# Attention scores of batches 2 to 7: three products of fp16 halves in place of one fp32 product

## The chip, the cores and the metric

The kernel runs on one core of a Trainium2 chip. The metric is the device time of one execution in microseconds (us), as the median of several runs. A profile of one more execution says what each engine did when. Engines are TensorE (PE; its weight loads are listed apart, as PEld), VectorE (DVE), ScalarE (ACT), GpSimd (POOL) and SyncE (SP, which issues the DMAs).

## The reference

Attention over a band of 65 keys and 32 global keys, with 32 global queries that see everything, is followed by a two-layer feed-forward part on all tokens. Cut to what matters:

```python
B, H, SL, SG, D = 8, 8, 512, 32, 64                       # inputs q_l, k_l, v_l, q_g, k_g, v_g
s_g   = q_g @ concat(k_g, k_l).T / 8                      # global queries, all 544 keys
out_g = softmax(s_g) @ concat(v_g, v_l)
s_ll  = where(|i - j| <= 32, q_l @ k_l.T / 8, -1e9)       # local queries, band
out_l = softmax(concat(q_l @ k_g.T / 8, s_ll)) @ concat(v_g, v_l)
x = concat(out_g, out_l).transpose(0, 2, 1, 3).reshape(B * 544, 512)
h = x @ w_in                                              # 512 -> 2048
out = (h * cos(h)) @ w_out                                # 2048 -> 512
```

The queries and keys are scaled up (factors 5.7 to 8), so the scores need more precision than one fp16 product gives.

## The kernel before

**Precision.** Nearly every product runs on PE as three products of fp16 halves: a value `x` is scaled by a power of two and split into `hi = fp16(x)` and `lo = fp16(x - hi)`, and `hi*hi + hi*lo + lo*hi` is summed in PSUM. The scores alone are single fp32 products (`sc_a`, L536, and `g_a`, L693).

**Tiling.** A batch has 4 head pairs, the two heads on partitions 0 to 63 and 64 to 127. Per pair, four windows of 128 queries see 192 or 224 keys each: `sc_a` computes windows 0 and 1 into two PSUM tiles (one per head), then windows 2 and 3 into two more, so a pair has two score blocks `ps_b_p_0_h` and `ps_b_p_2_h`, each of 4 matmuls with 64 rows of contraction. The global queries of two pairs are done together, in `gps_b_g_0` (288 keys) and `gps_b_g_1` (256 keys), 4 matmuls of 32 columns each.

**A pair's way.** SP loads queries and keys (`qkr_b_p`, three buffers); PE makes the scores `ps`; DVE scales them by -1/8, adds the mask and takes the row minimum (`sc_b`, tile `t`); ACT takes the exponential (`sc_c`); DVE the reciprocals (`sm`); ACT and DVE write the fp16 halves (`planes`, `sc_d`); SP transposes these by DMA (`pt`); PE multiplies them by the values (`acc`); ACT and DVE write the halves of the result (`xh`, `xl`).

**The feed-forward part** goes by chunks `c` of 256 tokens (two per batch) and 8 elements `j` per chunk: PE `ph_c_j` (24 matmuls of 256 columns), ACT `u`, DVE `u`, ACT `w` (sine), POOL `w*w`, DVE `gf`, ACT `gh` (fp16), POOL `gl` (the rest in fp16), and three elements later PE `po` (12 matmuls of 512 columns). There are three PSUM buffers for `ph`: `ph` of an element needs `gf` of the element three before it.

**Order.** `at(slot, phase, f, ...)` puts each step into a slot (one slot per element of the feed-forward part, 16 per batch); `steady` gives the slots of a pair of batches 2 to 7 relative to a slot `t`, which moves by 4 from pair to pair. A scheduler then orders each engine's instructions by these priorities. Every engine works through its own list strictly in order. In the names below, `ps_5_1_2_0` is batch 5, pair 1, windows 2 and 3, head 0; `u_8_4` is chunk 8, element 4. Attention of batch 5 runs beside the feed-forward part of batch 4 (chunks 8 and 9).

## Time and profile before

| what | value |
|---|---|
| three runs | 951.33, 949.33, 951.34 us (median 951.33) |
| the profiled execution's own time | 949.26 us |
| its span, first to last instruction | 947.5 us |
| PE / PEld / DVE / ACT / POOL busy | 95% / 63% / 61% / 70% / 45% |

The span is some 1.8 us shorter than the execution's own time; this lies outside of the instructions. Busy PE says that matmuls are in flight, not that the array is at its peak: matmuls overlap, so the cost of one is read from the distance between the starts of two.

### The profile page before, as it was taken

The numbers are of one execution on the slowest core, as the hardware profiler recorded it, in microseconds if no ns is written. First come the engines' busy times: TensorE is split into PE (matmuls) and PEld (weight loads), VectorE is DVE, ScalarE is ACT, GpSimd is POOL, SyncE is SP. The second block draws the span as 40 slices with busy tenths as digits, with TensorE's granted clock in tenths as the row PEclk, the third lists the DMA queues.
The fourth block names the chain that finished last, engine by engine and source line by source line (L and its number), as shares of the span: only waits on it lengthen the run. The fifth ranks groups of instructions, "written<-read, shape, count | busy, mean of one in ns | idle before, by whom it ended". The sixth has DMA issues, their size and how long they took to land.

```text
span 947.5 us, 19962 instructions
## 1 busy us (share of the span) xinstructions
PE 896.2 (95%) x7643; PEld 597.5 (63%) x7643; DVE 578.5 (61%) x1568; ACT 660.6 (70%) x1419; POOL 421.9 (45%) x508
## 2 busy tenths in 40 slices
...
GB/s 366 389 133 192 82 149 153 130 122 134 43 118 48 154 53 96 85 123 112 65 116 56 179 46 134 46 160 38 117 57 92 62 68 59 24 1 24 1 23 23
DMA packets 155176, 96.41 MB, mean 102 GB/s; under 512 B 141000, under 2 KB 141128, under 8 KB 153288
## 3 DMA queue, kind: packets, MB, share of 16 engines
...
## 4 chain that ended last, share of the span: by engine, by line
PE 82%; DVE 7%; ACT 3%; POOL 3%; DMA 2%; issue 1%; SPq 0%; ACTq 0%; POOLq 0%
PE ph L812 36%; PE po L872 35%; PE ps L536 5%; PE acc L654 4%; PE gps L693 2%; DVE planes L602 1%; PE gacc L748 1%; DMA raw_wo<-wo 1%; DMA vr<-v 1%; ACT t L434 1%; POOL wo_hl L222 1%; POOL vl L518 1%; DVE z_wo L241 1%; POOL wi_l L222 1%; DVE raw_wi L241 1%
## 5 line engine op out<-in xcount | busy, mean ns | idle before, releaser
L872 PE MATMUL po<-wo_hl,gh 128*128 128x512 f16 x1088 | 321.8, 380 | 9.7 <-POOL wo_hl L222 9.7
L812 PE MATMUL ph<-xh,wi_h 128*128 128x256 f16 x1024 | 280.4, 274 | 3.3 <-DVE gf L852 3.3
L812 PE MATMUL ph<-xl,wi_h 128*128 128x256 f16 x1024 | 279.8, 273 | 0.5 <-DVE xl L675 0.5
L812 PE MATMUL ph<-xh,wi_l 128*128 128x256 f16 x1024 | 279.8, 273 | 0.0
L222 POOL TENSOR_TENSOR gl<-gf,gh 128x512 f16<-128x512 f32 (+1 forms) x184 | 173.8, 955 | 230.2 <-ACT gh L856 229.3
L222 POOL TENSOR_TENSOR w<-w 128x512 f32<-128x512 f32 (+1 forms) x184 | 152.9, 841 | 248.3 <-ACT w L434 236.0
L812 PEld LDWEIGHTS <-wi_h 128*128 128x128 f16 x2176 | 206.0, 98 | 56.2 <-issue 19.6
L872 PE MATMUL po<-wo_hl,gl 128*128 128x512 f16 x544 | 201.5, 381 | 0.0
L872 PEld LDWEIGHTS <-gh 128*128 128x128 f16 x1088 | 106.8, 98 | 103.0 <-issue 2.3
L856 ACT CAST gh<-gf 128x512 f16<-128x512 f32 x136 | 83.3, 613 | 123.8 <-DVE gf L852 122.8
L852 DVE SCALAR_TENSOR_TENSOR gf<-w,ph 128x512 f32<-128x512 f32 x136 | 93.0, 684 | 113.7 <-POOL w L222 113.0
L434 ACT ACTIVATE w<-u,ca 128x512 f32<-128x512 f32 x136 | 97.9, 721 | 87.5 <-DVE u L835 84.8
L835 DVE SCALAR_TENSOR_TENSOR u<-u,cm,ph 128x512 f32<-128x512 f32 x136 | 101.2, 744 | 94.5 <-ACT u L834 94.5
L434 ACT ACTIVATE t<-t,mn 128x192 f32<-128x192 f32 (+1 forms) x256 | 116.6, 456 | 6.4 <-DVE mn L554 6.0
L812 PEld LDWEIGHTS <-wi_l 128*128 128x128 f16 x1088 | 106.7, 98 | 14.2 <-issue 1.4
L602 DVE SCALAR_TENSOR_TENSOR planes<-t,sm,planes 128x192 f16<-128x192 f32 (+1 forms) x232 | 100.4, 493 | 13.9 <-ACT planes L601 13.2
L834 ACT ACTIVATE u<-ph,cm 128x512 f32<-128x512 f32 x136 | 92.0, 677 | 18.8 <-PE ph L812 18.8
L872 PEld LDWEIGHTS <-gl 128*128 128x128 f16 x544 | 53.3, 98 | 73.0 <-issue 10.7
L554 DVE CUSTOM_DVE_ANT_0 t<-ps,msk 128x192 f32<-128x192 f32 (+1 forms) x256 | 82.8, 366 | 11.4 <-PE ps L536 10.4
L601 ACT ACTIVATE planes<-t,sm 128x192 f16<-128x192 f32 (+1 forms) x232 | 86.1, 455 | 2.2 <-DVE gsm L720 2.2
L536 PE MATMUL ps<-qkr 64*128 64x192 f32 (+1 forms) x496 | 73.0, 382 | 6.1 <-DMA qkr<-qf 5.4
L434 ACT ACT_TABLE_LOAD x58 | 74.4, 1283 | 3.7 <-DVE u L835 2.0
...
## 6 DMA issues: line engine op xcount, KB each, us to landing
qkr<-qf SPq DMA_DIRECT2D x31, 608.0 KB, 5.0
vr<-v SPq DMA_DIRECT2D x8, 1280.0 KB, 6.6
...
```

The lines of the kernel that those rows point to most:

```text
L222: nc.gpsimd.tensor_tensor(o[..., c], a[..., c], b[..., c], op=op)
L434: ins = nc.scalar.activation(*a, **k).ins
L536: nc.tensor.matmul(pt[h][:, c], q[r, QZ[j] : QZ[j] + P], k[r, z : z + w], start=True, stop=True, skip_group_check=True,)
L554: nc.vector.tensor_tensor_reduce(t[:, h], pt[h], msk[:, MOFF[i] : MOFF[i] + w], NAL, 3.0e38, ALU.add, ALU.min, mn[:, h : h + 1],)
L601: a = nc.scalar.activation(hi, t[:, h], AF.Identity, scale=r)
L602: d = nc.vector.scalar_tensor_tensor(lo, t[:, h], r, hi, op0=ALU.mult, op1=ALU.subtract)
L812: nc.tensor.matmul(ph[:, a], w[:, kc, f], x[:, kc, q], start=first and ip == 0, stop=last and ip == 2, skip_group_check=True,)
L834: nc.scalar.activation(u, ph, AF.Identity, bias=m)
L835: nc.vector.scalar_tensor_tensor(u, u, m, ph, op0=ALU.subtract, op1=ALU.subtract)
L852: nc.vector.scalar_tensor_tensor(gf, w, 0.5, st.pop(("ph", c, j)).rearrange("p a b -> p (a b)"), op0=ALU.subtract, op1=ALU.mult,)
L856: nc.scalar.copy(gh, gf)
L872: nc.tensor.matmul(po[k], g[:, a * CT + k * P : a * CT + (k + 1) * P], w[:, 2 * j + a], start=(j == 0 and i == 0), stop=(j == NS - 1 and i ...
```

## The change

For batches 2 to 7 the scores become three products of fp16 halves. What is added per pair:

- `q_m` (DVE): the largest absolute value per partition over queries and keys together, 1216 columns, into a bf16 column `qm`.
- `q_p` (PE): one matmul of that column with a constant matrix of ones. It sums the 128 maxima into a bound that all partitions get. It writes into one extra column of the PSUM tile of the score block two windows earlier, of the pair before (`host`), so it needs no PSUM tile of its own.
- `q_s` (DVE): five instructions on one column each, from the bound to a power-of-two scale and to the factor that takes the place of -1/8 in `sc_b` and `g_b`.
- `q_h`: ACT writes the upper half `qh` (1216 columns, fp16), DVE the lower half, in place over `qkr`.
- `sc_a` and `g_a`: three matmuls for one, the products outermost and the heads innermost.

The slots of a pair move: its load starts two slots earlier relative to `t` (-12 for -10), the first score block and the first global block one slot later (-6 for -7, -5 for -6), the load of the values one slot earlier (-13 for -12). The other new names in the diff (`SQ`, `GLE`, `WLE`, `WPT`, `WIS`, `PSQ`, `PSG`, `GB`, `LG`, `U1S`, `VDS`) hold what the expressions that they replace gave, and are left out here.

```diff
+FB = 2
+QB = 2
+QH = "A"
-s_load = -10
-s_sc0 = -7
+s_load = -12
+s_qm = -10
+s_qh = -8
+s_sc0 = -6
-s_gs0 = -6
+s_gs0 = -5
-s_v = -12
+s_v = -13
...
         def sc_a(b, p, i):
...
+            nb, np_ = (b, p + 1) if p < 3 else (b + 1, 0)
+            host = i == 2 and FB <= nb < B
+            pt = [
+                ps.tile([P, w0 + w1_ + (1 if host and h == 0 else 0)], F32, tag="att", name=f"ps_{b}_{p}_{i}_{h}")
+                for h in range(2)
+            ]
+            if host:
+                st["pmq", nb, np_] = pt[0][:, w0 + w1_ :]
+            if b >= FB:
+                qh, ql, kh, kl = st["qk", b, p]
+                for j, c in ((i, slice(0, w0)), (i + 1, slice(w0, w0 + w1_))):
+                    z, w = WIN[j]
+                    for n, (q, k) in enumerate(((qh, kh), (qh, kl), (ql, kh))):
+                        for h in range(2):
+                            r = slice(D * h, D * h + D)
+                            nc.tensor.matmul(
+                                pt[h][:, c], q[r, QZ[j] : QZ[j] + P], k[r, z : z + w], start=n == 0, stop=n == 2,
+                                skip_group_check=True,
+                            )
...
+        def q_m(b, p):
+            raw = st["raw_qk", b, p]
+            m = mp.tile([P, 1], BF16, tag="qm", name=f"qm_{b}_{p}")
+            nc.vector.tensor_reduce(
+                m, raw.rearrange("p a b -> p (a b)"), axis=AX.X, op=ALU.max, apply_absolute_value=True
+            )
...
+        def q_p(b, p):
+            nc.tensor.matmul(
+                st["pmq", b, p], ones13, st.pop(("qm", b, p)), start=True, stop=True, skip_group_check=True
+            )
...
+        def q_h(b, p):
+            raw, s = st.pop(("raw_qk", b, p)), st["qs", b, p][0]
+            hi = mp.tile([P, 2, NZ], F16, tag="qh", name=f"qh_{b}_{p}", bufs=QB)
...
+            if QH == "A":
+                nc.scalar.activation(hi, raw, AF.Identity, scale=s)
+            else:
+                nc.vector.tensor_scalar(hi, raw, s, None, op0=ALU.mult)
+            nc.vector.scalar_tensor_tensor(lo, raw, s, hi, op0=ALU.mult, op1=ALU.subtract)
...
         def attn_pair(b, p, o):
             if b:
                 at(o["load"], PJ, load_qk, b, p)
+            if b >= FB:
+                at(o["load"] + s_qm - s_load, PG, q_m, b, p)
+                h = o["host"]
+                at(h, PC, q_s, b, p)
+                at(max(h, o["load"] + s_qh - s_load), PF, q_h, b, p)
             attn_rest(b, p, o)
```

How the order of the engines moves is shown at three places, all while chunk 8 and the attention of batch 5 run.

PE, the first score block of pair 2 of batch 5. Before, from the last `po` matmul ahead of it to the `ph` behind it:

```order
L872 LDWEIGHTS gl_8_1_7009
L872 MATMUL po_8_1_7118<-wo_hl_88,gl_8_1_7009 128x512
L536 MATMUL ps_5_2_0_0_7242<-qkr_5_2_7005 128x192
L536 MATMUL ps_5_2_0_1_7243<-qkr_5_2_7005 128x192
L536 MATMUL ps_5_2_0_0_7242<-qkr_5_2_7005 128x224
L536 MATMUL ps_5_2_0_1_7243<-qkr_5_2_7005 128x224
L812 LDWEIGHTS wi_h_86
L812 MATMUL ph_8_5_7287<-xh_4_5803,wi_h_86 128x256
```

Now, the same place, the three products of its first window (192 columns):

```order
L969 MATMUL po_8_1_7631<-wo_hl_88,gl_8_2_7595 128x512
L558 LDWEIGHTS qh_5_2_7699
L558 MATMUL ps_5_2_0_0_7840<-qh_5_2_7699 128x192
L558 LDWEIGHTS qh_5_2_7699
L558 MATMUL ps_5_2_0_1_7841<-qh_5_2_7699 128x192
L558 LDWEIGHTS qh_5_2_7699
L558 MATMUL ps_5_2_0_0_7840<-qkr_5_2_7295,qh_5_2_7699 128x192
L558 LDWEIGHTS qh_5_2_7699
L558 MATMUL ps_5_2_0_1_7841<-qkr_5_2_7295,qh_5_2_7699 128x192
L558 LDWEIGHTS qkr_5_2_7295
L558 MATMUL ps_5_2_0_0_7840<-qh_5_2_7699,qkr_5_2_7295 128x192
L558 LDWEIGHTS qkr_5_2_7295
L558 MATMUL ps_5_2_0_1_7841<-qh_5_2_7699,qkr_5_2_7295 128x192
```

The three products of the second window follow in the same way, heads in turn. Then, in pairs 0 and 2, come the three products of window 2 for head 0 alone; those for head 1 follow only behind the next `ph` and `po`. The block now stands behind `ph_8_5`, where it stood ahead of it.

DVE, from the last `planes` of pair 1 of batch 5 to `gf_8_3`. Before:

```order
L602 SCALAR_TENSOR_TENSOR planes3_82<-t_5_1_2_7071,sm_5_1_7182,planes3_82 128x192 x2
L720 TENSOR_SCALAR gsm_5_0_7191<-gsm_5_0_7191 128x1
L721 RECIPROCAL gsm_5_0_7191<-gsm_5_0_7191 128x1
L730 TENSOR_SCALAR gt_5_0_6959<-gt_5_0_6959,gsm_5_0_7191 128x544
L731 CAST planes_g_84<-gt_5_0_6959 128x544
L835 SCALAR_TENSOR_TENSOR u_8_4_7226<-u_8_4_7226,cm_8_6817,ph_8_4_7201 128x512
L852 SCALAR_TENSOR_TENSOR gf_8_3_7197<-w_8_3_7114,ph_8_3_7088 128x512
```

Now, to `gf_8_4`:

```order
L582 TENSOR_REDUCE qm_5_3_7862<-qkr_5_3_7717 128x1
L679 SCALAR_TENSOR_TENSOR planes3_82<-t_5_1_2_7574,sm_5_1_7706,planes3_82 128x192
L615 SCALAR_TENSOR_TENSOR qkr_5_2_7295<-qkr_5_2_7295,qs_5_2_7584,qh_5_2_7699 128x1216
L582 TENSOR_REDUCE qm_6_0_8246<-qkr_6_0_8065 128x1
L808 TENSOR_SCALAR gsm_5_0_7715<-gsm_5_0_7715 128x1
L923 SCALAR_TENSOR_TENSOR u_8_4_7752<-u_8_4_7752,cm_8_7298,ph_8_4_7727 128x512
L946 SCALAR_TENSOR_TENSOR gf_8_3_7723<-w_8_3_7627,ph_8_3_7601 128x512
L809 RECIPROCAL gsm_5_0_7715<-gsm_5_0_7715 128x1
L923 SCALAR_TENSOR_TENSOR u_8_5_7824<-u_8_5_7824,cm_8_7298,ph_8_5_7799 128x512
L818 TENSOR_SCALAR gt_5_0_7581<-gt_5_0_7581,gsm_5_0_7715 128x544
L819 CAST planes_g_84<-gt_5_0_7581 128x544
L946 SCALAR_TENSOR_TENSOR gf_8_4_7795<-w_8_4_7753,ph_8_4_7727 128x512
```

Two reductions `qm` and the lower half (written to `qkr_5_2`) have come in ahead of `u_8_4` and `gf_8_3`, and `u_8_5` stands ahead of `gf_8_4`. On ACT the same stretch before:

```order
L434 ACTIVATE gt_5_0_6959,gsm_5_0_7191<-gt_5_0_6959,gmn_5_0_6960 128x544
L434 ACT_TABLE_LOAD
L434 ACTIVATE w_8_3_7114<-u_8_3_7113,ca_8_6816 128x512
L834 ACTIVATE u_8_4_7226<-ph_8_4_7201,cm_8_6817 128x512
L434 ACTIVATE w_8_4_7227<-u_8_4_7226,ca_8_6816 128x512
L856 CAST gh_8_3_7194<-gf_8_3_7197 128x512
L856 CAST gh_8_4_7280<-gf_8_4_7283 128x512
L834 ACTIVATE u_8_5_7312<-ph_8_5_7287,cm_8_6817 128x512
L434 ACTIVATE w_8_5_7313<-u_8_5_7312,ca_8_6816 128x512
L856 CAST gh_8_5_7331<-gf_8_5_7334 128x512
```

And now:

```order
L612 ACTIVATE qh_5_2_7699<-qkr_5_2_7295,qs_5_2_7584 128x1216
L448 ACTIVATE gt_5_0_7581,gsm_5_0_7715<-gt_5_0_7581,gmn_5_0_7582 128x544
L448 ACT_TABLE_LOAD
L448 ACTIVATE w_8_3_7627<-u_8_3_7626,ca_8_7297 128x512
L922 ACTIVATE u_8_4_7752<-ph_8_4_7727,cm_8_7298 128x512
L922 ACTIVATE u_8_5_7824<-ph_8_5_7799,cm_8_7298 128x512
L448 ACTIVATE w_8_4_7753<-u_8_4_7752,ca_8_7297 128x512
L950 CAST gh_8_3_7720<-gf_8_3_7723 128x512
L448 ACTIVATE w_8_5_7825<-u_8_5_7824,ca_8_7297 128x512
L950 CAST gh_8_4_7792<-gf_8_4_7795 128x512
L950 CAST gh_8_5_7865<-gf_8_5_7868 128x512
```

`qh_5_2` is new, and `u_8_5` has moved ahead of `w_8_4`, so that two elements are under way at a time.

DVE, where the maximum of the next batch's values (`vm_6`) is taken. Before:

```order
L554 ISA t_5_1_2_7071,mn_5_1_3_7075<-ps_5_1_2_0_7060,msk_73 128x192
L554 ISA mn_5_1_3_7075 128x1
L490 TENSOR_REDUCE vm_6_7583<-vr_6_7448 128x1
L852 SCALAR_TENSOR_TENSOR gf_8_2_7084<-w_8_2_7041,ph_8_2_7015 128x512
L554 ISA t_5_1_2_7071,mn_5_1_2_7072<-ps_5_1_2_1_7061,msk_73 128x224
L554 ISA mn_5_1_2_7072 128x1
L554 ISA t_5_1_2_7071,mn_5_1_3_7075<-ps_5_1_2_1_7061,msk_73 128x192
L554 ISA mn_5_1_3_7075 128x1
L462 TENSOR_SCALAR d_v6_7585<-ident_64,vm_6_7583 128x128
L835 SCALAR_TENSOR_TENSOR u_8_3_7113<-u_8_3_7113,cm_8_6817,ph_8_3_7088 128x512
```

Now:

```order
L594 TENSOR_SCALAR qs_5_2_7584<-ps_5_1_2_0_7541 128x1
L946 SCALAR_TENSOR_TENSOR gf_8_2_7597<-w_8_2_7522,ph_8_2_7496 128x512
L505 TENSOR_REDUCE vm_6_8041<-vr_6_7913 128x1
L794 ISA gt_5_0_7581,gmn_5_0_7582<-gps_5_0_0_7556,zero_74,ng_5_0_6834 128x288
L794 ISA gmn_5_0_7582 128x1
L488 TENSOR_SCALAR qs_5_2_7584<-qs_5_2_7584 128x1
L650 TENSOR_SCALAR sm_5_1_7706<-sm_5_1_7706 128x8
L923 SCALAR_TENSOR_TENSOR u_8_3_7626<-u_8_3_7626,cm_8_7298,ph_8_3_7601 128x512
L477 TENSOR_SCALAR d_v6_8043<-ident_64,vm_6_8041 128x128
```

`gf_8_2` stood behind `vm_6` and stands ahead of it now.

## Rows read from the trace of the kernel before

**Rows 1.** The page's part 1: busy us, share of the span and instructions of each engine.

```profile
PE 896.2 (95%) x7643; PEld 597.5 (63%) x7643; DVE 578.5 (61%) x1568; ACT 660.6 (70%) x1419; POOL 421.9 (45%) x508
```

**Rows 2.** Busy time by windows, from 203 to 710 us. Columns: window, its length, then PE, PEld, DVE, ACT and POOL busy (instructions), the granted clock of TensorE, DMA share, GB/s.

```profile
203.00:710.00 507.00, 507.00 (x4484) 335.82 (x4483) 313.99 (x880) 371.98 (x824) 189.82 (x173) 1.00 0.44 97
```

**Rows 3.** Who waited for whom in that window: total us, times, longest us.

```profile
ACT gh L856 <- DVE gf L852: 62.5, 40, 3.9
DVE gf L852 <- POOL w L222: 57.3, 50, 2.0
ACT w L434 <- DVE u L835: 55.3, 51, 2.8
...
ACT u L834 <- PE ph L812: 3.7, 2, 2.9
```

**Rows 4.** Instructions of PE in order of time (start us, duration us): the first `ph` matmuls of chunks 8 and 10, a batch apart; the second global block of pairs 0 and 1 of batch 6; the first matmul of `ph_10_6`.

```profile
501.71 0.28 PE L812 MATMUL ph<-xh,wi_h 128*128 128x256 f16 x1
...
603.19 0.28 PE L812 MATMUL ph<-xh,wi_h 128*128 128x256 f16 x1
...
629.22 0.64 PE L693 MATMUL gps<-qkr 128*32 128x256 f32 x8
...
641.23 0.27 PE L812 MATMUL ph<-xh,wi_h 128*128 128x256 f16 x1
```

**Rows 5.** Instructions of DVE in order of time: `gf` of element 3 in chunks 8 and 10.

```profile
538.31 0.68 DVE L852 SCALAR_TENSOR_TENSOR gf<-w,ph 128x512 f32<-128x512 f32 x1
...
640.33 0.68 DVE L852 SCALAR_TENSOR_TENSOR gf<-w,ph 128x512 f32<-128x512 f32 x1
```

**Rows 6.** PE in order of time around fp32 scores: a global block and a score block, each with its neighbours. An fp32 matmul is two records.

```profile
411.77 0.38 PE L872 MATMUL po<-wo_hl,gl 128*128 128x512 f16 x1
412.08 0.69 PE L693 MATMUL gps<-qkr 128*32 128x288 f32 x8
412.70 0.22 PE L748 MATMUL gacc<-ptg,vh 128*64 128x64 f16 x2
...
418.01 0.59 PE L872 MATMUL po<-wo_hl,gh 128*128 128x512 f16 x2
418.44 0.38 PE L872 MATMUL po<-wo_hl,gl 128*128 128x512 f16 x1
418.75 0.97 PE L536 MATMUL ps<-qkr 64*128 64x224 f32 x8
419.66 0.28 PE L812 MATMUL ph<-xh,wi_h 128*128 128x256 f16 x1
```

**Rows 7.** PE in order of time, short fp16 matmuls, each with a weight load of its own: eight transposes (128 columns loaded, 128 streamed), products with the values (64 columns loaded, two heads side by side in the array).

```profile
75.28 0.61 PE L618 MATMUL tr<-ident,planes 128*128 128x128 f16 x8
...
413.00 0.19 PE L748 MATMUL gacc<-ptg,vl 128*64 128x32 f16 x2
413.04 0.20 PE L748 MATMUL gacc<-ptg,vh 128*64 128x64 f16 x2
...
527.23 0.33 PE L654 MATMUL acc<-pt,vh 128*64 128x192 f16 x4
527.40 0.25 PE L654 MATMUL acc<-pt,vl 128*64 128x192 f16 x2
```

**Rows 8.** Groups of instructions by line and shape in the window 203 to 710: busy us, mean ns of one, idle time before them.

```profile
L520 ACT ACTIVATE vh<-vr,vs 128x640 f16<-128x640 f32 x20 | 15.9, 818 | 5.0 <-DVE vs L473 4.9
...
L601 ACT ACTIVATE planes<-t,sm 128x224 f16<-128x224 f32 x76 | 30.1, 468 | 0.0
...
L835 DVE SCALAR_TENSOR_TENSOR u<-u,cm,ph 128x512 f32<-128x512 f32 x80 | 59.6, 744 | 41.9 <-ACT u L834 41.9
L852 DVE SCALAR_TENSOR_TENSOR gf<-w,ph 128x512 f32<-128x512 f32 x79 | 54.1, 684 | 57.9 <-POOL w L222 57.3
...
L490 DVE TENSOR_REDUCE vm<-vr 128x1 f32<-128x2560 f32 x5 | 14.1, 2820 | 14.8 <-DMA vr<-v 14.8
```

**Rows 9.** DVE in order of time: the first of four `t` of a score block and the instruction behind the four; two lower halves of values (640 columns). POOL works beside the second and not beside the first.

```profile
562.51 0.34 DVE L554 CUSTOM_DVE_ANT_0 t<-ps,msk 128x192 f32<-128x192 f32 x1
...
563.69 0.28 DVE L500 TENSOR_REDUCE vs<-pm_v 128x1 f32<-128x128 f32 x1
...
570.03 0.88 DVE L521 SCALAR_TENSOR_TENSOR vl<-vr,vs,vh 128x640 f16<-128x640 f32 x1
...
571.02 1.59 DVE L521 SCALAR_TENSOR_TENSOR vl<-vr,vs,vh 128x640 f16<-128x640 f32 x1
```

**Rows 10.** ACT in order of time, from `gh_8_2` to the first exponential of pair 2 of batch 5; what ended the idle time before an instruction stands in brackets.

```profile
528.80 0.62 ACT L856 CAST gh<-gf 128x512 f16<-128x512 f32 x1 [3.48 <-DVE gf L852]
...
534.18 0.73 ACT L434 ACTIVATE gt<-gt,gmn 128x544 f32<-128x544 f32 x1
...
541.09 0.62 ACT L856 CAST gh<-gf 128x512 f16<-128x512 f32 x1 [1.37 <-DVE gf L852]
...
545.76 0.62 ACT L856 CAST gh<-gf 128x512 f16<-128x512 f32 x1 [1.87 <-DVE gf L852]
...
549.88 0.46 ACT L434 ACTIVATE t<-t,mn 128x192 f32<-128x192 f32 x1
```

**Rows 11.** DMA issues of the page (KB each, median us from issue to landing).

```profile
qkr<-qf SPq DMA_DIRECT2D x31, 608.0 KB, 5.0
vr<-v SPq DMA_DIRECT2D x8, 1280.0 KB, 6.6
```

More of the change, by code (lines that the diff above doesn't have):

```diff
@@ L47 @@
 SPLIT = 256
+LG = 3
+LGC = 2
+GB = 4
 PL = 1
@@ L73 @@
 L7 = -5
-PS = 128
+PSQ = 128
+PSG = 128
+SQ = "GGGGGGGGGGGGGGGG"
+GLE = "GGGGGGGGGGGGGGGG"
+WLE = "GGGGGGGGGGGGGGGG"
+WPT = [1, 1, 2, 2, 3, 3, 4, 4, 5, 5, 6, 6, 7, 7, 8, 8]
+WIS = 256
+U1S = [2, 4, 6, 8]
+VDS = [1, 2, 3, 4]
 MR = 2
@@ L451, in load_qk @@
             st["qk", b, p] = (t[:, 0], t[:, 1])
+            st["raw_qk", b, p] = t
         def load_v(b):
@@ L526, in sc_a @@
                 return
+            w0, w1_ = WIN[i][1], WIN[i + 1][1]
+            nb, np_ = (b, p + 1) if p < 3 else (b + 1, 0)
[17 more added lines that the diff above has]
+                            )
+                    st["ps", b, p, j] = [t[:, c] for t in pt]
+                if host:
+                    q_p(nb, np_)
+                return
             q, k = st["qk", b, p]
-            w0, w1_ = WIN[i][1], WIN[i + 1][1]
-            pt = [
-                ps.tile([P, w0 + w1_], F32, tag="att", name=f"ps_{b}_{p}_{i}_{h}") for h in range(2)
-            ]
             for j, c in ((i, slice(0, w0)), (i + 1, slice(w0, w0 + w1_))):
@@ L540, in sc_a, with q_s @@
                 st["ps", b, p, j] = [t[:, c] for t in pt]
+            if host:
+                q_p(nb, np_)
+        def q_m(b, p):
[4 more added lines that the diff above has]
+            )
+            st["qm", b, p] = m
+        def q_p(b, p):
+            nc.tensor.matmul(
+                st["pmq", b, p], ones13, st.pop(("qm", b, p)), start=True, stop=True, skip_group_check=True
+            )
+        def q_s(b, p):
+            m = mp.tile([P, 4], F32, tag="qs", name=f"qs_{b}_{p}", bufs=3)
+            nc.vector.tensor_scalar(m[:, 0:1], st.pop(("pmq", b, p)), 2.0**-53, None, op0=ALU.max)
+            scale_of(m[:, 1:2], m[:, 0:1])
+            pow2(m[:, 0:1], m[:, 0:1])
+            nc.vector.tensor_scalar(m[:, 2:3], m[:, 0:1], m[:, 0:1], NAL / 4, op0=ALU.mult, op1=ALU.mult)
+            if p % 2 == 0:
+                st["ng", b, p // 2] = mp.tile([P, 1], F32, tag="ng", name=f"ng_{b}_{p}")
+            r = slice(64 * (p % 2), 64 * (p % 2) + 64)
+            nc.vector.tensor_scalar(
+                st["ng", b, p // 2][r], m[r, 0:1], m[r, 0:1], NAL / 4, op0=ALU.mult, op1=ALU.mult
+            )
+            st["qs", b, p] = (m[:, 1:2], m[:, 2:3])
+        def q_h(b, p):
+            raw, s = st.pop(("raw_qk", b, p)), st["qs", b, p][0]
+            hi = mp.tile([P, 2, NZ], F16, tag="qh", name=f"qh_{b}_{p}", bufs=QB)
+            flat = raw.rearrange("p a b -> p (a b)")
+            lo = flat.bitcast(F16)[:, : 2 * NZ].rearrange("p (a b) -> p a b", a=2)
+            if QH == "A":
[3 more added lines that the diff above has]
+            nc.vector.scalar_tensor_tensor(lo, raw, s, hi, op0=ALU.mult, op1=ALU.subtract)
+            st["qk", b, p] = (hi[:, 0], lo[:, 0], hi[:, 1], lo[:, 1])
         def sc_b(b, p, i):
@@ L690, in g_a @@
             for hh in range(4):
+                if b >= FB:
+                    break
                 q, k_ = st["qk", b, 2 * g + hh // 2]
```

39 lines of the change are left out of this document (28 added, 11 removed).

## The prediction

> **What bounds the kernel now.** The first view is the page: PE is 95% busy, ACT 70%, DVE 61% [rows 1]. The second is busy time by windows: from 203 to 710 us, while batches 2 to 7 have their attention, PE is busy 507 of 507 us at a granted clock of 1.00, which is 2.4 GHz, with ACT at 73%, DVE at 62% and POOL at 37% [rows 2]. So in this stretch work taken from PE is time, if the others keep up. The third view, the waits, tells whether they can. ACT waits 62.5 us for DVE's `gf` and 55.3 us for DVE's `u`, DVE 57.3 us for POOL's squares, but ACT only 3.7 us for PE's `ph` [rows 3]. The other engines lose their idle time to one another, not to PE. Their round through one batch is a second clock beside PE's, and instructions in order of time give both: the first `ph` of chunks 8 and 10 start at 501.71 and 603.19, so PE takes 101.5 us per batch [rows 4]; `gf` of element 3 in the same chunks starts at 538.31 and 640.33, so the round takes 102.0 us [rows 5]. The round falls behind, and `gf_10_3`, over at 641.01, comes only 0.2 us ahead of `ph_10_6` at 641.23, which needs its buffer [rows 4, 5]. A gain on PE therefore counts only as far as the round becomes shorter too. That is the heart of the case, since the change adds work to the round.
>
> **PE, score blocks.** Ahead of the fp32 block the `po` matmul starts at 418.44, the block at 418.75, the next `ph` at 419.66 [rows 6]. From 418.75 that is 0.91 us, and the step into the block is 0.31 us, where two `po` records take 0.43 (418.01 to 418.44), 0.22 each, so 0.09 more: 1.00 us per block, 48 blocks, 48.0 us. In fp16 two heads' products should run side by side, since they use different halves of the rows, as the fp32 ones do. The nearest row is `acc`, where two heads also run side by side: two pairs of 192 columns take 527.40 - 527.23 = 0.17 us, 0.085 per pair [rows 7]; for 224 columns that scales to 0.099. Three products of each are 0.55 us, and 0.03 for the step: 0.58 per block. In pairs 0 and 2 the order shows window 2 with its heads one behind the other: three products of 0.099 more, 0.88 per block. With 36 blocks of the first kind and 12 of the second this is 31.4 us: 16.6 saved.
>
> The bounds. The lower one is the one taken, since columns have to be streamed. For the upper one no overlap at all is assumed: 12 products, 1.10 us, 53 us, 5 more than now. Between them lies the price of a weight load: eight transposes, each loading 128 columns, take 0.61 us, at most 0.076 each [rows 7], which gives 0.91 per block; but `gacc` and its load of 64 columns follow each other two in 0.04 us [rows 7], so two loads of 128 columns fit into 0.08. That is nearest, and so is the lower bound.
>
> The Trainium skill's page "TensorE: Matmul & The Clock Gate", section "Back-to-back issue gap", speaks against the change: pairs of a weight load and a matmul of 128 columns are said to sustain about 81 ns each, set by both. By it twelve products take 0.97 us, the score blocks save 1.4 us in all, the 24 global ones lose 7 and `q_p` 2, and the kernel is slower by some 8 us, an estimate of 957. The rows above do not agree: side by side, such pairs take half of that.
>
> **PE, global blocks.** 0.72 us for 288 keys (412.70 - 412.08, and 0.10 for the step) [rows 6]; for 256 keys by columns 0.64; 12 of each, 16.3 us. Three products at the rate of `acc` (0.44 ns per column) and a step of 0.03 are 0.41 and 0.37, 9.4 us: 6.9 saved. The 24 `q_p`, one column each behind a load of 128, I put at 0.06 each, 1.4 us. PE saves 16.6 + 6.9 - 1.4 = 22.1 us, 3.7 per batch: 97.8 us where it was 101.5.
>
> **What is added to the round, per pair.** `qm` reduces 1216 columns; `vm` takes 2.82 us for 2560 [rows 8], so 1.35. The lower half goes by `vl`: 0.88 us for 640 columns alone and 1.59 beside POOL [rows 9], so 1.5 or 3.0; POOL has nothing to do where the order puts it, so 1.5. `qh` on ACT: 0.468 us for 224 columns and 0.818 for 640 [rows 8], so 1.3. Five small instructions, some 0.15 each. Per batch DVE gets 14.4 us, ACT 5.2. The sum of busy time allows that (DVE 62 to 79%); where it stands decides.
>
> *Elements 3 to 6 of each chunk.* Before, ACT's `planes` end at 534.18, `gf_8_3` starts at 538.31 (4.1 later), the exponentials at 549.88 (15.7 later) [rows 5, 10]. Now `qm`, the lower half and `qm` stand ahead of `u_8_4` and `gf_8_3`. DVE's `planes` end about two of ACT's (0.47 each [rows 8]) after ACT's, 0.9; with 1.35 + 1.5 + 1.35 and `u` 0.74 [rows 8] `gf_8_3` starts at 5.8, so 1.7 later. `gf_8_4` gets `u_8_5` (0.74) ahead of it, and about half of that lies beside POOL's square: 0.4 more. Against that, `gh_8_4` to `gh_8_5` took 545.76 - 541.09 = 4.67 us, because elements 4 and 5 went strictly one behind the other, with waits of 1.37 and 1.87 for `gf` [rows 10]. With `u_8_5` ahead of `w_8_4` both are under way, and between the two `gf` DVE has four `t` (562.51 to 563.69, 1.2 us [rows 9]) and a `gf` (0.68), 1.9 us: 2.8 less. Balance -0.7. Behind the exponentials `qh_5_3` adds 1.3 on ACT; its lower half hides behind the table load. So +0.6, twice per batch: +1.2.
>
> *Elements 0 and 1* are interlaced in the same way (`w_8_1` now stands ahead of `gh_8_0`); as the halves of the values stand between, I take 2.1 for the 2.8, twice: -4.2. *`vm`*: before, `gf_8_2` stood behind it and its load, and ACT waited 3.48 us for it ahead of the last exponentials [rows 10]. Now the exponentials run through, but `sm` and the `planes` still stand behind `vm`, so that only 1.2 comes back. The round: 102.0 + 1.2 - 4.2 - 1.2 = 97.8 us, level with PE's 97.8.
>
> *A new wait.* `qm_5_3` needs its load, which needs the buffer that the second global block frees. From that block to `ph_x_6` PE has 641.23 - 629.22 = 12.0 us [rows 4], 11.3 from the block's end and with the shorter score block. In these the load has to land (5.0 us [rows 11]), and DVE has to go through `qm`, the lower half, `qm`, `u` and `gf_x_3` (1.35 + 1.5 + 1.35 + 0.74 + 0.68 = 5.6, and 0.5 for a `planes` between). 11.1 just fits. If the two loads issued there take as long as one of 1280 KB, 6.6 us [rows 11], 1.4 is missing, twice per batch. On DVE's queue everything of the feed-forward part stands behind this `qm`.
>
> **Sum.** The profiled execution took 949.3 us. The period falls from 101.5 to 97.9 (the longer of the two clocks and 0.1 for their friction), six batches: -21.6. In the lead-in, where DVE is full, `qm_2_0`, and `qm_2_2` behind a load, cost 1 to 3: +2. That gives 929.7, so 930. The profiled execution is 2 us below the median shown, within what runs differ by; I don't add it.
>
> **Rivals.**
> *A, PE keeps the pace or nearly (930).* Chance 0.58; own range 922 to 937.
> *B, the new wait at `qm` (942).* Loads of 6.6 us: 97.8 + 2.8 = 100.6 per batch, 0.9 saved six times, and 2 lost in the lead-in: 946; half of that lateness gives 938. For: SP issues the two loads back to back. Against: the median of 5.0 already has such pairs in it. Chance 0.20, price midway.
> *C, the round does not shorten (slower, 988).* If the interlacing brings nothing, because the waits only move to POOL's squares, the round is 102.0 + 2 x (1.7 + 0.4 + 1.3) - 1.2 = 107.6; PE has 0.2 us in hand [rows 4, 5], so 6.1 x 6 = 37 us more and the 2 of the lead-in: 988. It decides from a round of 101.5 on. Against: the order plainly takes out the serial places. 0.12.
> *D, the products don't overlap.* 53 us for score blocks: PE saves 0.5 us and the lead-in costs 2, 951; with loads at the transposes' price (0.91 per block, 43.7 us) it saves 9.8, 942. 0.10. This is also the case where the change doesn't do what it says. The Trainium skill's rule above goes further in the same direction.
>
> **Numbers.** Within 0.2% (2 us) is about what a measurement can't tell from no change. Faster: A, nearly all of B and half of D, 0.58 + 0.19 + 0.06 = 0.83; the same: 0.05; slower: C 0.12. From 921 (A's lower end) to 948 (B, most of D) lie 0.84 of the chances.
>
> **What would show it.** Right: score blocks of 0.6 and 0.9 us, global ones below 0.4; the first `ph` of chunks 8 and 10 at 97 to 99 us apart; `gf` in the same step. B would show as waits of DVE `qm` for the DMA `qkr`, followed by PE `ph` waiting for `gf`; C as PE `ph` or `ps` waiting for DVE with no DMA behind it; D as blocks near 1 us with PE still at 100%. The prediction is wrong if the count of the round misses a queue: each microsecond per batch is six.

## The result, and the profile after

The changed kernel takes 961.91 us (median; 959.34 to 966.22), the kernel before 950.57 in the same session (949.33 to 951.34): a ratio of 1.0129, 95% interval 1.0113 to 1.0144. Forecast were 930 us and a range of 921 to 948. The prediction was wrong: the kernel became slower.

The page of the changed kernel, part 1 (busy us, share of the span, instructions) and part 4 (the chain that ended last, by engine and by line):

```profile
PE 888.2 (93%) x7955; PEld 598.9 (63%) x7955; DVE 675.2 (71%) x1736; ACT 686.2 (72%) x1443; POOL 425.1 (44%) x508
...
PE 35%; DVE 21%; ACT 9%; issue 6%; DMA 4%; POOL 0%; ACTq 0%; SPq 0%; DVEq 0%; POOLq 0%
```

Part 4 of the kernel before:

```profile
PE 82%; DVE 7%; ACT 3%; POOL 3%; DMA 2%; issue 1%; SPq 0%; ACTq 0%; POOLq 0%
```

Against [rows 1] PE has 8 us less, DVE 97 more, ACT 26 more. In the chain of the kernel before PE had 82%; now DVE and ACT have 30% of it: PE is no longer the bound. The same by window, as in [rows 2] (PE, PEld, DVE, ACT, POOL busy, granted clock, DMA share, GB/s):

```profile
203.00:710.00 507.00, 487.70 (x4629) 329.02 (x4628) 391.78 (x1008) 385.11 (x826) 192.71 (x174) 0.99 0.43 97
```

PE, busy in all 507 us before, now stands idle for 19. Who waited for whom in that window, as in [rows 3]:

```profile
ACT w L448 <- DVE u L923: 49.8, 46, 2.2
ACT gh L950 <- DVE gf L946: 43.8, 26, 5.5
...
DVE vm L505 <- DMA vr<-v: 14.7, 5, 4.2
...
PE gps L781 <- DVE xg L852: 12.0, 5, 2.5
DVE qkr L615 <- ACT qh L612: 11.8, 9, 1.3
...
ACT L448 <- DVE u L923: 10.0, 9, 1.1
...
PE ph L900 <- DVE gf L946: 6.0, 5, 1.4
...
DVE gf L946 <- POOL w L236: 5.4, 11, 0.7
...
DVE qm L582 <- DMA qkr<-qf: 1.1, 2, 0.8
```

New or grown are these: PE waits for DVE (12.0 us in the global block, which waits until `xg` has read the PSUM buffer, and 6.0 us in `ph`, which waits for `gf`), DVE's lower half (written over `qkr`) for ACT's `qh`, and ACT's table load for DVE's `u`, 10.0 us, where it was 2.0. DVE waited for POOL's squares 57.3 us before [rows 3] and now 5.4. DVE went from the engine that waits to the engine that is waited for.

**The period.** `gf` of element 3 in chunks 8 and 10 (DVE in order of time):

```profile
547.02 0.68 DVE L946 SCALAR_TENSOR_TENSOR gf<-w,ph 128x512 f32<-128x512 f32 x1
...
651.72 0.67 DVE L946 SCALAR_TENSOR_TENSOR gf<-w,ph 128x512 f32<-128x512 f32 x1
```

104.7 us, against 102.0 in [rows 5]. From the starts of `gf` of element 0, the mean of the four steps from chunk 4 to chunk 12 is 103.2 (102.0 before), where 97.9 was forecast. Over the run `gf` of element 0 in chunk 2 starts 1.5 us later than before, the next period (batch 2 into 3) is 6.3 longer, the four behind it 4.6 together, and the last is 2.4 shorter: 10.0 of the 10.1 us between the two profiled spans (947.5 and 957.6).

**TensorE's clock.** The granted clock of 0.99 in the window above is 1.00 but for two stretches, by windows as above; behind them PE's row ahead of the first:

```profile
271.00:275.00 4.00, 4.00 (x31) 2.74 (x24) 3.82 (x16) 3.51 (x9) 1.04 (x1) 0.57 0.25 87
581.50:585.50 4.00, 4.00 (x24) 2.88 (x22) 3.28 (x15) 3.97 (x11) 1.04 (x1) 0.57 0.17 66
...
270.83 0.31 PE L781 MATMUL gps<-qh 128*32 128x288 f16 x4 [2.37 <-DVE xg L852]
```

For most of these 4 us the granted clock was the lower level, 1.2 GHz, and `ph` matmuls followed each other in 0.21 us in place of 0.11. Both stretches came just behind a wait of 2.4 us for `xg`; PE waited as long for it at three other places, and no fall came there. The step to `gf` of element 3 that holds such a stretch took 16.3 us in chunk 3 and 15.8 in chunk 9, and 14.2 in each of chunks 5, 7 and 11. So 3.7 of the 10.1 us of this execution go with the clock. In no other run's trace did the clock fall between 203 and 710 us. The other executions of the changed kernel were up to 7 us longer than the profiled one; whether the clock fell more often in them isn't shown.

**PE did get its gain.** A score block between a `po` and `gacc`, a global block of 256 keys between `acc` and `ph`, and the end of the first score block of pair 0, up to `ph`, as in [rows 6]:

```profile
417.08 0.38 PE L969 MATMUL po<-wo_hl,gl 128*128 128x512 f16 x1
417.39 0.26 PE L558 MATMUL ps<-qh 64*128 64x192 f16 x2
...
418.03 0.22 PE L836 MATMUL gacc<-ptg,vh 128*64 128x64 f16 x2
...
431.93 0.29 PE L781 MATMUL gps<-qh 128*32 128x256 f16 x4
...
432.37 0.28 PE L900 MATMUL ph<-xh,wi_h 128*128 128x256 f16 x1
...
496.35 0.26 PE L558 MATMUL ps<-qh 64*128 64x224 f16 x2
...
496.64 0.26 PE L558 MATMUL ps<-qh 64*128 64x224 f16 x1
...
497.02 0.28 PE L900 MATMUL ph<-xh,wi_h 128*128 128x256 f16 x1
```

A global block of 256 keys in the kernel before:

```profile
426.27 0.64 PE L693 MATMUL gps<-qkr 128*32 128x256 f32 x8
426.84 0.28 PE L812 MATMUL ph<-xh,wi_h 128*128 128x256 f16 x1
```

Twelve products take 0.64 us (0.73 with the step of 0.09) where the fp32 block took 0.91 (1.00); the global block takes 0.44 where it took 0.57. In pairs 0 and 2, where three products of head 0 stand alone at the end of the first block, its fifteen take 0.93, and the nine that are left in the second take 0.64: 1.57 for the pair, where it is 1.28 with the heads in turn. Three products of one head take as long as six of both (496.35 to 496.64, 0.29 us, and 0.93 - 0.64), so the heads do run side by side. Per pair of weight load and product twelve in 0.64 us are 53 ns. The Trainium skill's page "TensorE: Matmul & The Clock Gate", section "Back-to-back issue gap", gives about 81 ns per matmul for a stream of such pairs at 128 columns; with two heads side by side the trace does not agree, and the measurement decides.

**Where DVE's time stands.** DVE in order of time through the stretch that the prediction walked, from `gf_8_2` to `u_8_7`; what ended the idle time before an instruction is in brackets:

```profile
530.59 0.68 DVE L946 SCALAR_TENSOR_TENSOR gf<-w,ph 128x512 f32<-128x512 f32 x1
533.78 2.82 DVE L505 TENSOR_REDUCE vm<-vr 128x1 f32<-128x2560 f32 x1 [2.51 <-DMA vr<-v]
...
539.49 2.51 DVE L679 SCALAR_TENSOR_TENSOR planes<-t,sm,planes 128x192 f16<-128x192 f32 x7
541.93 1.41 DVE L582 TENSOR_REDUCE qm<-qkr 128x1 bf16<-128x1216 f32 x1
...
543.58 1.48 DVE L615 SCALAR_TENSOR_TENSOR qkr<-qkr,qs,qh 128x1216 f16<-128x1216 f32 x1
544.98 1.41 DVE L582 TENSOR_REDUCE qm<-qkr 128x1 bf16<-128x1216 f32 x1
...
546.37 0.73 DVE L923 SCALAR_TENSOR_TENSOR u<-u,cm,ph 128x512 f32<-128x512 f32 x1
547.02 0.68 DVE L946 SCALAR_TENSOR_TENSOR gf<-w,ph 128x512 f32<-128x512 f32 x1
...
548.34 0.99 DVE L818 TENSOR_SCALAR gt<-gt,gsm 128x544 f32<-128x544 f32 x1
549.37 1.28 DVE L819 CAST planes_g<-gt 128x544 f16<-128x544 f32 x1
550.57 0.67 DVE L946 SCALAR_TENSOR_TENSOR gf<-w,ph 128x512 f32<-128x512 f32 x1
...
557.24 0.69 DVE L946 SCALAR_TENSOR_TENSOR gf<-w,ph 128x512 f32<-128x512 f32 x1 [0.48 <-POOL w L236]
...
562.88 1.49 DVE L615 SCALAR_TENSOR_TENSOR qkr<-qkr,qs,qh 128x1216 f16<-128x1216 f32 x1 [1.31 <-ACT qh L612]
564.28 0.74 DVE L923 SCALAR_TENSOR_TENSOR u<-u,cm,ph 128x512 f32<-128x512 f32 x1
```

Four things stand here one behind the other: `vm` with its wait (5.3 us); `qm`, lower half and `qm`, without a gap, ahead of `u_8_4` and `gf_8_3`; the global rows' division and cast (2.3 us) between `gf_8_3` and `gf_8_4`; and a lower half that waits 1.31 us for ACT, with `u_8_7` behind it. ACT at the last of these:

```profile
561.54 1.30 ACT L612 ACTIVATE qh<-qkr,qs 128x1216 f16<-128x1216 f32 x1
562.75 0.67 ACT L922 ACTIVATE u<-ph,cm 128x512 f32<-128x512 f32 x1
...
565.10 1.28 ACT L448 ACT_TABLE_LOAD   x1 [1.11 <-DVE u L923]
566.39 0.72 ACT L448 ACTIVATE w<-u,ca 128x512 f32<-128x512 f32 x1
```

ACT's `u` is done at 563.42, DVE's only at 565.02, because the lower half stands ahead of it; table load and `w` wait for that.

Durations by line and shape in the window, first of the changed kernel, then of the kernel before (busy us, mean ns, idle before):

```profile
L631 DVE CUSTOM_DVE_ANT_0 t<-ps,msk,qs 128x224 f32<-128x224 f32 x78 | 33.2, 443 | 0.0
...
L819 DVE CAST planes_g<-gt 128x544 f16<-128x544 f32 x10 | 12.8, 1278 | 0.3
...
L818 DVE TENSOR_SCALAR gt<-gt,gsm 128x544 f32<-128x544 f32 x10 | 9.9, 994 | 0.0
```

```profile
L554 DVE CUSTOM_DVE_ANT_0 t<-ps,msk 128x224 f32<-128x224 f32 x80 | 30.6, 383 | 2.2 <-PE ps L536 2.1
...
L730 DVE TENSOR_SCALAR gt<-gt,gsm 128x544 f32<-128x544 f32 x10 | 5.0, 504 | 0.3
L731 DVE CAST planes_g<-gt 128x544 f16<-128x544 f32 x10 | 4.4, 444 | 0.3
```

`t` takes 60 ns more with its scalar read from a column; the division and the cast take 1.3 us more together at their new place.

### The profile page after: what moved, and what is told of

Same layout as the page of the kernel before. It is cut to its first block, busy times and chain, and to the rows that moved or that the text cites. A ratio compares the mean times of both kernels' runs of the same rounds, so it can differ in the third digit from the quotient of the medians.

```text
span 957.6 us, 20771 instructions
## 1 busy us (share of the span) xinstructions
PE 888.2 (93%) x7955; PEld 598.9 (63%) x7955; DVE 675.2 (71%) x1736; ACT 686.2 (72%) x1443; POOL 425.1 (44%) x508
## 4 chain that ended last, share of the span: by engine, by line
PE 35%; DVE 21%; ACT 9%; issue 6%; DMA 4%; POOL 0%; ACTq 0%; SPq 0%; DVEq 0%; POOLq 0%
PE po L969 16%; PE ph L900 16%; DVE planes L679 5%; DVE u L923 3%; ACT t L448 3%; DMA vr<-v 3%; DVE qkr L615 3%; DVE qm L582 2%; DVE gf L946 2%; DVE t L631 2%; ACT planes L678 2%; DVE vl L536 1%; DMA qkr<-qf 1%; ACT qh L612 1%; PE acc L731 1%
## 5 line engine op out<-in xcount | busy, mean ns | idle before, releaser
L236 POOL TENSOR_TENSOR gl<-gf,gh 128x512 f16<-128x512 f32 (+1 forms) x184 | 175.8, 966 | 211.6 <-ACT gh L950 211.2
L900 PEld LDWEIGHTS <-wi_h 128*128 128x128 f16 x2176 | 208.8, 99 | 57.5 <-issue 17.5
L678 ACT ACTIVATE planes<-t,sm 128x192 f16<-128x192 f32 (+1 forms) x232 | 86.1, 455 | 12.9 <-issue 7.7
L631 DVE CUSTOM_DVE_ANT_0 t<-ps,msk,qs 128x192 f32<-128x192 f32 (+1 forms) x192 | 71.5, 427 | 0.3 <-PE ps L558 0.3
L448 ACT ACTIVATION_READ_ACCUMULATOR t<-t,mn 128x1 f32 x256 | 48.1, 188 | 0.0
```

The source lines that it names most:

```text
L236: nc.gpsimd.tensor_tensor(o[..., c], a[..., c], b[..., c], op=op)
L448: ins = nc.scalar.activation(*a, **k).ins
L631: nc.vector.tensor_tensor_reduce(t[:, h], pt[h], msk[:, MOFF[i] : MOFF[i] + w], nal, 3.0e38, ALU.add, ALU.min, mn[:, h : h + 1],)
L678: a = nc.scalar.activation(hi, t[:, h], AF.Identity, scale=r)
L900: nc.tensor.matmul(ph[:, a], w[:, kc, f], x[:, kc, q], start=first and ip == 0, stop=last and ip == 2, skip_group_check=True,)
```

## The experiments

Each was run in five rounds beside the kernel before. An edge is an added rule that one instruction of an engine has to stand behind another in its order. Ratios are to that kernel, with 95% intervals. "Less" is said against the changed kernel's 961.9 (ratio 1.0129); the kernel before took 949.6 to 950.6 in all four sessions, so that times of different ones can be set side by side to about 1 us.

**1. The moved slots alone.**

```diff
-FB = 2
+FB = 8
```

> The changed kernel with the fp16 scores turned off for every batch (the first batch to use them is set to 8, and there are eight, 0 to 7): the fp32 scores of the kernel before, with only the moved slots (load two slots earlier, scores of windows 0 and 1 and the first global block one later, values one earlier). Theory 1 (the slots are harmless, and it is the added work on VectorE and ScalarE that holds the round at 102 to 103 us per batch): TensorE still needs 101.5 us per batch and stays the bound, so 949 to 953 us. Rival 2 (the moved slots themselves lengthen the round, because the values' maximum now stands in front of its load and the scores come later): 955 to 962 us, with TensorE waiting for VectorE's gf.

951.7 us, ratio 1.0020 [1.0011, 1.0030]. The slots cost 2 us at most; the period is 102.2. Rival 2 falls.

**2. Three products, with halves made once.**

```diff
-                at(o["load"] + s_qm - s_load, PG, q_m, b, p)
-                at(h, PC, q_s, b, p)
...
+            if (b, p) == (FB, 0):
...
+                nc.scalar.activation(hi, raw, AF.Identity, scale=1.0)
+                nc.vector.scalar_tensor_tensor(lo, raw, 1.0, hi, op0=ALU.mult, op1=ALU.subtract)
+                st["halves"] = (hi[:, 0], lo[:, 0], hi[:, 1], lo[:, 1])
+            st["qk", b, p] = st["halves"]
...
-            nal = st["qs", b, p][1] if b >= FB else NAL
+            nal = NAL
...
```

> The changed kernel without the added work of the round: maximum, scale, the copy to fp16 and the low half are made once, for the first pair of batch 2, and every later pair multiplies these same halves, so the scores are not those of its own data; the mask pass takes a constant scale, and TensorE has the three fp16 products as before, without the one-column sums. Theory 1: TensorE becomes the bound at what its own stretches in the changed kernel give, 2.0 us per batch less than before (12 products from first to next instruction 0.64 us against 0.91 for the fp32 block, global ones 0.44 against 0.57), so 949.3 - 12 = 937, up to 941. Rival 2 (slots): 948 to 958, since the slots stay. Rival 3 (the forecast's block costs are right after all and the waits hide it): 930 or below.

941.3 us, ratio 0.9916 [0.9900, 0.9931], at the edge of what theory 1 gave, but not by its working: from 305 to 710 us PE is busy throughout and a period is 98.3 us, 3.2 less than before and not 2.0. The rest is lost in the lead-in, where `gf` of element 0 in chunk 2 comes 6.3 us later than before; in this kernel nothing waits for the later loads any more, and what that does to the lead-in was not looked into.

**3. Without the lower half.**

```diff
-            nc.vector.scalar_tensor_tensor(lo, raw, s, hi, op0=ALU.mult, op1=ALU.subtract)
-            st["qk", b, p] = (hi[:, 0], lo[:, 0], hi[:, 1], lo[:, 1])
+            st["qk", b, p] = (hi[:, 0], hi[:, 0], hi[:, 1], hi[:, 1])
```

> The changed kernel without the low halves: VectorE's instruction that makes them is left out, and the second and third product take the high halves again, so the scores lack what the low halves add. TensorE's work is the same. Theory 1: 24 instructions of 1.49 us and their wait for ScalarE's copy (15.4 us in all) leave VectorE's queue; about half of that stands on the path of the round, 3 us per batch, so 942 to 948 us. Rival 2 (slots): 957 to 962.

934.7 us, ratio 0.9839 [0.9825, 0.9853], 27 us less than the changed kernel and more than expected. Its window from 305 to 710:

```profile
305.00:710.00 405.00, 405.00 (x3911) 273.21 (x3908) 298.59 (x829) 323.62 (x692) 158.57 (x141) 1.00 0.45 98
```

PE is the bound again, at 98.6 us per batch (three of four periods; one is 97.8). So 24 instructions of 1.5 us on DVE, with their waits for ACT, decide whether PE's gain arrives. TensorE has the same products here but not in quite the same order: in every block of the window the heads take turns, as in experiments 2 and 4, so the 0.29 us that pairs 0 and 2 have more in the changed kernel are gone as well.

**4. Without the maximum over queries and keys.**

```diff
-            nc.vector.tensor_reduce(
-                m, raw.rearrange("p a b -> p (a b)"), axis=AX.X, op=ALU.max, apply_absolute_value=True
-            )
+            nc.vector.memset(m, 4.0)
```

> The changed kernel without the maximum over queries and keys: a constant bound is written in its place by an instruction on one column, everything behind it (sum on TensorE, scale, copy to fp16, low half) stays. Theory 1: 24 instructions of 1.41 us leave VectorE's queue; where two of them stand with a low half between planes and u, their 2.8 us lie on the path once per batch, and half of the others, so 3 us per batch and 942 to 948 us. Rival 2 (slots): 957 to 962.

945.1 us, ratio 0.9950 [0.9938, 0.9962], as theory 1 expected; a period is 100.2 us.

**5. Constant scalar in the mask pass.**

```diff
-            nal = st["qs", b, p][1] if b >= FB else NAL
+            nal = NAL
...
-                t[:, c0 : c0 + w], st.pop(("gps", b, g)), zero[:, :w], st["ng", b, g] if b >= FB else NAL,
+                t[:, c0 : c0 + w], st.pop(("gps", b, g)), zero[:, :w], NAL,
...
```

> The changed kernel with the constant scalar of the kernel before in the mask pass and in the global one, where the change reads it from a column in memory; the scale is still worked out, but its effect on the exponents is left out, so the scores are scaled wrongly. All engines keep their order but for a few neighbours. Theory 1 (VectorE's work counts wherever it stands): t takes 366 ns in place of 427, 192 times, and gt about 56 ns less, 24 times, 13 us in all, 2.2 per batch, so some 950 us. Rival 2 (only what stands ahead of a waiting instruction counts; the t stand between two gf, where PoolE's square is waited for anyway): 956 to 962 us.

951.7 us, ratio 1.0019 [1.0007, 1.0030]: 10 us for 192 times 60 ns and 24 times some 60 (12.9 us). The instruction in the window:

```profile
L631 DVE CUSTOM_DVE_ANT_0 t<-ps,msk 128x224 f32<-128x224 f32 x80 | 29.1, 383 | 0.0
```

The same 383 ns as before the change. But not all of the 10 us is DVE's work: between the two profiled executions lie 9.1 us, and 3.7 of them go with the clock, which did not fall here. The 5.4 that are left are about two fifths of the work taken off DVE. So neither theory is borne out as it stands.

**6. Lower half behind `u`.** An edge in the order; the same work.

```diff
...
+            tc.add_manual_dep(ins, st["last_u"].name, order, reason="low_after_u")
...
```

> The changed kernel with one edge more in the order: the low half of a pair stands behind VectorE's next u in place of ahead of it. That moves 11 of the 24 low halves by one place, all of them such as waited for ScalarE's copy while u, and behind it the table load and Sin, waited for them; nothing is left out. Theory 2 (place counts: work and wait ahead of u are on the path): 11 times 1.49 us and the wait of 1.3 go from the path, less what the low half takes from the instruction behind it, so 15 to 30 us less: 935 to 947 us. Theory 1 (the sum of VectorE's work counts): 958 to 962 us.

951.5 us, ratio 1.0021 [1.0011, 1.0032]: 10 us less, between the two theories. Place counts, but the step from `gf` of element 6 to that of element 7 lost only 0.8 us, not 2.8: the lower half now delays what stands behind it.

**7. `vm` four elements later.**

```diff
...
+                if b >= 2:
+                    tc.add_manual_dep(ins, st["last_gf"].name, order, reason="values_after_gf")
...
```

> The changed kernel with one edge more in the order: the values' maximum vm of batches 2 to 7 stands behind gf of element 6 (four elements later), where VectorE then has 2.5 us of idle time, in place of behind gf of element 2, where it waited for its load with u, the softmax sums and all planes of a pair behind it; nothing is left out. Theory 2 (place counts): the wait of 2.5 to 4.2 us and the 2.8 us of vm leave the path once per batch, of which the other chain through ScalarE gives back part: 3 us times 6, so 941 to 948 us. Rival: the wait was as long in the kernel before (14.8 us against 14.7) and cost nothing there, so 958 to 962 us.

943.2 us, ratio 0.9929 [0.9917, 0.9941]: 19 us less than the changed kernel. The period is 99.9.

**8. Both.**

> Both edges together: low half behind u, vm behind gf of element 6. If both stand on the path and TensorE's bound is the 98.6 us per batch that the run without low halves showed, 933 to 939 us; if the sum of VectorE's work counts, 955 to 962.

943.9 us, ratio 0.9933 [0.9918, 0.9947]: neither. The two don't add. Part of what is left stands on PE, in whose queue the sum of the values' maximum now waits for a step of DVE (window 203 to 710):

```profile
PE pm_v L483 <- DVE qs L209: 4.6, 5, 1.4
```

**9. The global rows' division later.**

```diff
-s_gd = -3
+s_gd = -1
...
+            tc.add_manual_dep(ins, st["last_gf"].name, order, reason="global_after_gf")
...
```

> The changed kernel with one edge more in the order: the division of the global rows (gt by gsm) and its cast planes_g stand behind gf of element 5, in place of between gf of elements 3 and 4; nothing else moves on VectorE, and on PoolE the low half of planes_g alone. In the changed kernel the two take 0.99 and 1.28 us there, because PoolE squares at the same time; in the kernel before, ahead of u of element 4, 0.50 and 0.44. Theory 2 (place counts): 2.2 us between the two gf leave the path twice per batch and go to a place where VectorE waits 1.3 us for ScalarE's u, where they cost 0 to 1; 1.2 to 2.2 us twice per batch, so 937 to 948 us. Rival (the two gf wait for PoolE's squares anyway): 957 to 962 us.

946.1 us, ratio 0.9959 [0.9947, 0.9971]: 16 us less, for twelve moved pairs of instructions. The cast at its new place (minimum, median, maximum ns):

```profile
L820 DVE CAST planes_g<-gt x10: 443/444/445, 245.8 to 695.1; 128x544 f16<-128x544 f32 x10
```

It is back at 444 ns (the division takes 776 in the mean), and `gf` of element 4 follows that of element 3 by 2.05 us where it was 3.54, in both chunks of a batch.

**10. `vm` later in the kernel before.**

> The kernel before with vm of batches 2 to 7 behind a later gf (by the slots of the kernel before it comes behind gf of element 7); nothing else is changed. The same move brought 18.7 us in the changed kernel. If TensorE bounds the kernel before at 101.5 us per batch, with a round of 102.0 that just follows, the gain is at most 0.5 per batch: 945 to 950 us. If the round was the bound in the kernel before as well, 2.5 to 3 us per batch: 930 to 936 us.

951.0 us, ratio 0.9998 [0.9988, 1.0007]. Window 203 to 710:

```profile
203.00:710.00 507.00, 507.00 (x4485) 335.99 (x4483) 313.34 (x889) 372.65 (x830) 189.03 (x176) 1.00 0.44 97
```

The move that brought 19 us behind the change brings nothing ahead of it. PE bounds the kernel before. The time is 1 us above the range that was expected: the first five periods are some 0.5 us shorter each, the most that was expected, but `gf` of element 0 in chunk 2 comes 2.2 us later and the last period is 1.6 longer.

**11 and 12. Three edges, and four.** 11 is 7 and 9 together, with the matmul that sums the values' maximum one slot later; 12 adds the edge of 6.

```diff
-            at(t + s_v + 1, PG, v_b, b)
-            at(t + s_v + 1, PG2, v_c, b)
+            at(t + s_v + 2, PG, v_b, b)
+            at(t + s_v + 2, PG2, v_c, b)
```

> The changed kernel with vm behind gf of element 6, the sum of the values' maximum on TensorE and what follows it one slot later (there TensorE waited for VectorE, 4.9 us in all, once vm stood later), and the global rows' division behind gf of element 5; nothing is left out. If these places are what the forecast missed, TensorE is at its own bound of 98.6 us per batch: 933 to 938 us. If low half and maximum of queries and keys keep the round above that: 939 to 943.

> As the run before, and the low half of 11 pairs behind u. If the round is below TensorE's bound already: the same as the run before within 1 us. If not: 2 to 6 us less than it.

937.2 us, ratio 0.9861 [0.9846, 0.9876], and 937.4, ratio 0.9867 [0.9854, 0.9880]. Both are faster than the kernel before and than the changed one. Three edges, window 305 to 710:

```profile
305.00:710.00 405.00, 404.82 (x3896) 273.88 (x3895) 323.06 (x842) 323.23 (x688) 158.86 (x140) 1.00 0.46 100
```

PE is busy to within 0.2 us, and a period is 99.2, 0.6 more than without lower halves. No wait accounts for these 0.6, but PE's order does: here as in the changed kernel the two blocks of pairs 0 and 2 take 0.93 and 0.64 us, without lower halves 0.64 each, which is 2 times 0.29 per batch. DVE has 7 us more of work in these 405 us than in the changed kernel (315.7 there), because more of the kernel passes in them; it is no longer in the way. The fourth edge adds nothing, since the round is then below PE's bound.

## Why the prediction was wrong

**PE's saving: right in kind, 1.4 us per batch too high.** 3.7 us per batch were forecast. In the changed kernel's order the period at which PE is the bound (experiment 11) gives 101.5 - 99.2 = 2.3; with the heads in turn in all blocks (experiment 3) it is 101.5 - 98.6 = 2.9. The blocks in the rows above give somewhat less, 8 times 0.27 and 4 times 0.13, 2.7, less 2 times 0.29. The products lie side by side, as taken from `acc` [rows 7], but at 0.64 us for twelve, not 0.55, and with a step of 0.09, not 0.03. The 0.30 that the forecast added where one head's products stand behind the other's is what was measured, 0.29. Rival D falls. (The lower end of rival A's range stands in the prediction as 922 and as 921; nothing hangs on it.)

**The round: the step that failed.** The count said 102.0 - 4.2 = 97.8 us. It became 103.2. The starts of all `gf` of chunks 4 to 11 (attention of batches 3 to 6), put in order, give the mean step from each to the next, and the forecast's terms can be held against them (us per batch, change against the kernel before; even and odd chunk of a batch apart where two numbers stand):

| place | forecast | measured |
|---|---|---|
| `gf_2` and `gf_3`, even chunk (`vm`, and `qm`, lower half, `qm`) | +1.7 - 1.2 | -5.59 + 6.33 = +0.74 |
| `gf_3`, odd chunk | +1.7 | +2.10 (+1.71 in the three chunks without the fall of the clock) |
| `gf_3` to `gf_4` | +0.4, +0.4 | +1.49, +1.50 |
| `gf_4` to `gf_5`, interlaced | -2.8, -2.8 | -2.66, -2.66 |
| `gf_6` to `gf_7`, behind the exponentials | +1.3, +1.3 | +2.05, +2.02 |
| elements 0 and 1, interlaced (odd chunk: with the step to `gf_2`) | -2.1, -2.1 | -1.49, -2.37 |
| the rest | 0 | +0.43 |
| sum | -4.2 | +1.1 |

The interlacing came as forecast, and so did the price of `qm` and lower half ahead of `gf_3`. 0.4 of the 5.3 us between the two sums is the fall of TensorE's clock in chunk 9, which the forecast did not have: it kept the granted clock of [rows 2]. Three more costs were missed.

- *`gf_3` to `gf_4`, 2.2 of the 5.3 us.* "`gf_8_4` gets `u_8_5` (0.74) ahead of it" overlooked what else the order puts there: the global rows' division and cast, which had stood ahead of `u_8_4`. It was a move of work that the change doesn't name, and at the new place the two take 2.27 us for 0.95. POOL at that time:

```profile
547.99 1.04 POOL L236 TENSOR_TENSOR w<-w 128x512 f32<-128x512 f32 x1 [1.65 <-ACT w L448]
548.99 1.35 POOL L236 TENSOR_TENSOR gl<-gf,gh 128x512 f16<-128x512 f32 x1
```

  POOL's instructions end at 549.03 and 550.34, DVE's division and cast at 549.33 and 550.65 by their starts and durations (548.34 + 0.99, 549.37 + 1.28): each 0.3 us behind POOL's end, as if it had stood still until then; the same 0.30 stands in all ten places of the window. Experiment 9 shows the price: 16 us. The Trainium skill's page "SBUF — State Buffer", section "A bandwidth-pool intuition that's wrong (but worth ruling out)", says that a GpSimd instruction and a VectorE one that uses both ports can't work at the same time, and that one then blocks fully; these rows agree, though no run here shows which ports the two use.
- *Behind the exponentials, 1.5 us.* "Its lower half hides behind the table load" was wrong in its direction: the table load waits for `u`, and `u` stands behind the lower half, which waits for ACT's `qh`. ACT's rows above show it; experiment 6 shows 10 us for it.
- *The scalar of `t`.* The prediction gave `t` its old duration. 32 times 60 ns are 1.9 us per batch; experiment 5 gives back 10 us, of which its trace shows 1.1 us per batch in the steps to `gf_2` and `gf_5` of both chunks, and 3.7 us in all with the clock.

These prices don't add to one loss. Taken away one at a time, the lower half's work, its place, the maximum, `vm`'s place, the division's place and the scalar bring 27, 10, 17, 19, 16 and 10 us; all that can be had is some 25, down to PE's bound of 99.2 (27 where the heads take turns in all blocks). Any one of them shortens a round that stands some 4 us per batch above that bound. And in the trace of each the clock did not fall, which alone is 3.7 us of the changed kernel's profiled execution. Why `vm`'s place brings 3.3 us per period, when it takes 2.5 off the step to `gf_3`, is seen in part: the step from `gf_6` to `gf_7` in the even chunk became 1.0 shorter too, though `vm` now stands there. What shortened it was not pursued.

**The lead-in: +2 forecast.** +1.5 to the first `gf` of chunk 2, as expected, but the first period behind it was 108.3 us, 5.1 more than the later ones. Two places hold this. The step to `gf_3` in chunk 3 took 16.3 us, 2.1 more than where the clock did not fall. And the steps from `gf_0` to `gf_3` of chunk 2 took 27.2 us, 3.5 more than the mean of the later even chunks; there `vm` stands ahead of `gf_1`, behind a wait of 4.2 us for its load. The runs show that it goes with the rest (101.6 without lower halves, 99.6 with three edges).

**The rivals.** B, `qm` waiting for its load, is refuted: 1.1 us of waits in the whole window. C was right in direction and in its sign to look for, PE waiting for DVE with no DMA behind it, but priced at 988 and with a chance of 0.12. It took the interlacing for lost. The truth lay between A and C: the interlacing came, and other work moved in its place. The round was counted to 97.8, exactly PE's forecast, so the forecast had nothing in hand. Of the 29.7 us between its -19.6 and the measured +10.1, the six periods hold 30.1 (-21.6 forecast, +8.5 measured) and the lead-in -0.5; with a shorter round, PE's own 1.4 per batch would still have kept some 8 of them.

**What held.** With the order mended (experiment 11) the same work takes 937.2 us, inside the forecast's range: 2.2 us lost in the lead-in, as forecast, 2.8 us gained in each of five periods and 0.9 in the last, where 3.6 were forecast for each.
